# FNet mixer on one core: the reads of the third and seventh block products stand in a row on VectorE, and the work for the other token half moves behind the second group's weight sums

## The chip, the cores and the metric

The kernel runs on one core of a Trainium2 chip. The metric is the device time of one execution in microseconds (us). The time before is the median of three runs, 673.58 us (673.05 to 673.78). The profile is of one further execution, which took 673.93 us from start to end; the span from its first to its last instruction is 672.2 us, so 1.73 us lie around the span.

## The reference, cut to what matters

```python
xn = _layernorm(x)                        # x: 2048 tokens x 512
a = einsum("bsd,ed->bse", xn, hid_re)     # DFT along the hidden axis
b = einsum("bsd,ed->bse", xn, hid_im)
s = einsum("ts,bse->bte", seq_re, a) - einsum("ts,bse->bte", seq_im, b)
y = _layernorm(xn)
h = gelu(einsum("bsd,df->bsf", y, w1) + b1)     # 512 -> 1792
g = silu(einsum("bsf,fd->bsd", h, w2) + b2)     # 1792 -> 512
return x + s * g
```

All inputs are fp32. The kernel writes an fp32 factor as a rounded high part and a rest (`hi`, `lo`) and forms each product as three matmuls: high by high, high by rest, rest by high.

## The kernel before, in words

The program is one stream of calls in a fixed order. Each engine (TensorE, VectorE, ScalarE, GpSimd and the DMA queue of SyncE) takes its own instructions in the order in which the calls were written, and waits on semaphores where an operand is missing or a buffer is still being read. So where a call stands in the code sets what stands ahead of it on its engine.

It has four stages, one behind the other on TensorE: the DFT along the hidden axis (to some 95 us of the span), the first MLP layer (`h_product`, line 646), the second MLP layer (`m_product`), and the DFT along the sequence (`multiply_by`). The change lies in the last part of the first stage and at the start of the second.

**The block products of the first stage.** The 2048 tokens are four blocks of 512. For blocks 2 and 3 the hidden DFT is done in the manner of Strassen and Winograd: seven block products p in the order 1, 2, 5, 6, 3, 7, 4, written by `q_product` (line 540). Each has four chunks c of 128 tokens, and a chunk is six matmuls into one PSUM accumulator: `qy`, `qx` or `qz`, by p. Products 1, 6, 7 and 4 of one chunk share the accumulator `qy`. Behind products 1, 5, 6 and 4 ScalarE copies the accumulator out (line 520); behind 2, 3 and 7 VectorE adds it to what was copied before (line 525, called by `post`). These reads must be over before the next product adds to the same accumulator: chunk c of product 4 waits for VectorE's read of chunk c of product 7.

`q_product` takes one list of steps for each chunk. They are calls for what later work needs, and are written behind the chunk: the next group's weights and the token operands of the first MLP layer.

**The weights.** The first MLP layer also uses seven products, for each of seven weight groups j. `w1_load` brings a group by DMA into `w1r`, `w1_sums` (lines 437 to 440) makes four sums in place on VectorE, `w1_round` (444) makes the high parts on ScalarE and `w1_rest` (83) the rests on VectorE. There is one buffer for `w1r`, so the load of group j+1 waits for the rests of group j. Loads 1 and 2 are issued by GpSimd.

**The token operands.** They are seven per token half tau: "11", "12", "21", "22" and the sums t1 to t4, for tau 1 (blocks 2 and 3, used in the block products too) and tau 0 (blocks 0 and 1). `y_scale` (461) scales one on VectorE, `y_sum` (475) makes a sum in place on VectorE, `y_round` (79) rounds on ScalarE and `y_rest` (83) makes the rest on VectorE.

**The start of the first MLP layer.** `h_seq` sets the order: groups 0 and 1 with tau 1 alone, then both with tau 0, then the other groups with both halves. With (j, p) for group and product, the first thirteen are (0,1), (0,5), (0,6), (0,2), (0,3), (0,7), (1,1), (1,5), (0,4), (1,6), (1,2), (1,3), (1,7), each six matmuls; the next, (0,1) with tau 0, is the first that reads a token operand of tau 0. Products 1, 6, 7 and 4 of a group share the accumulator `hy`, and 5 and 3 share `hz`. Behind 1, 5 and 6 ScalarE copies the accumulator out (`hc`, `hu`, line 671); behind 2, 3 and 7 VectorE adds it (lines 700, 706, 710) and ScalarE applies the GELU (660). `y_late` lists the calls that are written ahead of a given product of this order; the key's last number is tau.

## Time and profile before

| | |
|---|---|
| median of three runs | 673.58 us (673.05 to 673.78) |
| the profiled execution | 673.93 us |
| its span | 672.2 us |
| mean granted TensorE clock | 0.995 |
| bytes moved by DMA | 172.28 MB |
| sequence-DFT loads `c<-ct` by SyncE | 68 of 512 KB, 5.8 us each |

The rows of TensorE are modelled: a matmul's row is 0.39 us long, while the next starts 0.23 us behind it, so the distance from start to start is what counts. A row of the timeline holds its start and its length in us, the engine, the source line, the operation, out<-in, and in brackets the idle time ahead of it and what ended it.

### The profile page before, as it was taken

The page shows a single profiled execution, that of the slowest core. Times are in us where ns is not written, and L with a number is a line of the kernel's source. Part 1 is how long each engine was busy: PE and PEld are TensorE (multiplying, and loading weights), DVE is VectorE, ACT ScalarE, POOL GpSimd, SP SyncE. Part 2 cuts the span into 40 slices and gives each one's busy share as a digit, 9 for nine tenths or more (in the row PEclk, how much of TensorE's full clock was granted, in tenths as well). Part 3 has the DMA queues.
Part 4 walks back from the last instruction along what each step waited for, and adds up shares of the span by engine and source line. Part 5 has one row for each costly group of instructions (what it writes and reads, how often), then busy time and mean ns, then how long its engine had stood idle before and what let it go on. Part 6 is the DMA issues. An engine that isn't in the chain of part 4 may idle for free.

```text
span 672.2 us, 8165 instructions
## 1 busy us (share of the span) xinstructions
PE 663.4 (99%) x2908; PEld 544.5 (81%) x2908; DVE 544.0 (81%) x592; ACT 355.1 (53%) x395; POOL 50.7 (8%) x84
## 2 busy tenths in 40 slices
PE   9999989999999999999999999999999999999996
PEld 5888877888888888888888888888888888888885
DVE  7999886667778856987888999729978299998985
ACT  4745656544555665555456455446445455646540
POOL 1001000222112100000000100000000001210100
PEclk9999989999999999999999999999999999999999
DMA  8879260597998999798799997416555558996873
GB/s 319 268 250 231 94 233 1 221 332 273 331 341 302 417 417 362 261 394 292 276 376 409 390 324 255 157 34 206 182 155 142 128 126 264 302 258 255 294 253 126
DMA packets 70329, 172.28 MB, mean 256 GB/s; under 512 B 6640, under 2 KB 21008, under 8 KB 70288
## 3 DMA queue, kind: packets, MB, share of 16 engines
q1 hardware_dynamic: 57904, 131.36, 55.4%
q0 software_dynamic: 12032, 39.86, 18.9%
q10 hardware_dynamic: 352, 0.54, 0.3%
q8 instruction: 23, 0.38, 0.2%
q14 instruction: 18, 0.15, 0.1%
HBM read 121.38 MB, written 50.35 MB: 255 GB/s over the span
## 4 chain that ended last, share of the span: by engine, by line
PE 93%; DVE 4%; ACT 1%; issue 1%; DMA 0%; DVEq 0%; ACTq 0%
PE pz L841 19%; PE px L841 18%; PE ma L841 11%; PE hy L655 11%; PE mb L841 8%; PE pd L338 6%; PE hz L655 5%; PE pw L841 5%; PE hx L655 3%; PE px L1160 2%; PE pw L1160 2%; PE qy L537 1%; PE pd L353 1%; DVE q L525 1%; DVE xT L475 1%
## 5 line engine op out<-in xcount | busy, mean ns | idle before, releaser
L947 DVE TENSOR_TENSOR c<-c,c 128x1024 f32<-128x1024 f32 x32 | 39.0, 1219 | 4.4 <-DMA c<-ct 4.4
L65 DVE TENSOR_TENSOR R_b1l<-c,R_b1h 128x1024 fp32r<-128x1024 f32 x16 | 19.5, 1222 | 13.7 <-ACT R_b1h L64 10.4
L660 ACT ACTIVATE hc<-hc,b_t 128x1024 f32<-128x1024 f32 (+1 forms) x18 | 17.3, 962 | 24.7 <-DVE hc L700 19.7
L64 ACT ACTIVATE R_s3h<-c 128x1024 fp32r<-128x1024 f32 x16 | 17.0, 1061 | 24.2 <-DVE c L947 15.9
L841 PE MATMUL pw<-R_s1h,L 128*128 128x512 f32 x96 | 29.7, 389 | 0.0
L83 DVE TENSOR_TENSOR w1l<-w1r,w1h 128x1792 fp32r<-128x1792 f32 x7 | 14.2, 2024 | 18.3 <-ACT w1h L444 18.3
L64 ACT ACTIVATE R_b2h<-c 128x1024 fp32r<-128x1024 f32 x16 | 16.9, 1057 | 22.0 <-DVE c L952 17.5
L65 DVE TENSOR_TENSOR R_s2l<-c,R_s2h 128x1024 fp32r<-128x1024 f32 x16 | 19.6, 1223 | 8.6 <-PE pz L841 8.6
L64 ACT ACTIVATE R_s2h<-c 128x1024 fp32r<-128x1024 f32 x16 | 17.0, 1060 | 16.7 <-PE px L841 9.3
L65 DVE TENSOR_TENSOR R_s3l<-c,R_s3h 128x1024 fp32r<-128x1024 f32 x16 | 19.5, 1219 | 3.8 <-PE pz L841 3.8
L64 ACT ACTIVATE R_s1h<-c 128x1024 fp32r<-128x1024 f32 x16 | 16.4, 1051 | 11.3 <-DVE c L958 11.3
L955 POOL DMA_DIRECT2D c<-ct x8 | 7.0, 875 | 200.7 <-DVE c L952 162.5
L64 ACT ACTIVATE R_b1h<-c 128x1024 fp32r<-128x1024 f32 x16 | 16.6, 1052 | 10.1 <-PE px L841 4.4
L64 ACT ACTIVATE R_a1h<-c 128x1024 fp32r<-128x1024 f32 x16 | 16.9, 1054 | 8.9 <-PE pz L841 7.2
L841 PEld LDWEIGHTS pw<-R_s1h,L 128*128 128x128 f32 x96 | 18.0, 188 | 3.8
L65 DVE TENSOR_TENSOR R_b2l<-c,R_b2h 128x1024 fp32r<-128x1024 f32 x16 | 19.4, 1218 | 1.5 <-PE px L841 1.5
L65 DVE TENSOR_TENSOR R_a1l<-c,R_a1h 128x1024 fp32r<-128x1024 f32 x16 | 19.5, 1221 | 1.3 <-PE px L841 1.1
L952 DVE TENSOR_TENSOR c<-c,c 128x1024 f32<-128x1024 f32 x16 | 19.6, 1222 | 0.4
L65 DVE TENSOR_TENSOR R_s4l<-c,R_s4h 128x1024 fp32r<-128x1024 f32 x16 | 19.5, 1219 | 0.5 <-PE px L841 0.4
L64 ACT ACTIVATE R_s4h<-c 128x1024 fp32r<-128x1024 f32 x16 | 16.8, 1050 | 4.8 <-PE pz L841 2.9
L65 DVE TENSOR_TENSOR R_s1l<-c,R_s1h 128x1024 fp32r<-128x1024 f32 x16 | 18.8, 1219 | 0.1
L64 ACT ACTIVATE w2h<-w 128x1024 fp32r<-128x1024 f32 (+1 forms) x14 | 13.2, 943 | 10.8 <-DVE w L768 3.9
(950 smaller groups left out, 2221.3 us busy)
## 6 DMA issues: line engine op xcount, KB each, us to landing
c<-ct SPq DMA_DIRECT2D x68, 512.0 KB, 5.8
m<-h_d SPq DMA_DIRECT2D x48, 512.0 KB, 6.8
h_d<-ht POOLq DMA_DIRECT2D x21, 512.0 KB, 6.1
s_d<-sa SPq DMA_DIRECT2D x32, 256.0 KB, 3.9
la<-s_d SPq DMA_DIRECT2D x32, 256.0 KB, 6.1
h_d<-hc POOLq DMA_DIRECT2D x13, 512.0 KB, 3.6
x<-x SPq DMA_DIRECT2D x16, 256.0 KB, 4.7
sa<-a_d SPq DMA_DIRECT2D x8, 512.0 KB, 5.8
```

The costliest lines, as they stand in the source:

```text
L64: nc.scalar.activation(hi, src, AF.Copy)
L65: nc.vector.tensor_sub(lo, src, hi.bitcast(F32))
L83: nc.vector.tensor_sub(hi_lo[1], src, hi_lo[0].bitcast(F32))
L338: nc.tensor.matmul(acc, xt[i, k][px], weights[m * NK + k][pw], start=n == 0, stop=n == len(terms) - 1)
L353: nc.tensor.matmul(dacc[0, m], xt[0, k][px], weights[m * NK + k][pw], start=seen[m] == 0, stop=seen[m] == 3 * NK - 1)
L655: nc.tensor.matmul(acc[:, tau, :], w[:, W1_AT[p], k * P:(k + 1) * P], r[:, k, :], start=p in (1, 5, 2) and i == 0, stop=p in (2, 3, 4) and ...
L660: nc.scalar.activation(dst, src, AF.Gelu_apprx_tanh, bias=b1_t[:, row:row + 1])
L841: nc.tensor.matmul(acc[k][:, tau, :], a, c[:, tau, :], start=first and i == 0, stop=last and i == len(terms) - 1, skip_group_check=True)
L947: nc.vector.tensor_sub(t, t, raw)
L952: nc.vector.tensor_add(raw, raw, t)
L955: nc.gpsimd.dma_start(out=t, in_=ct[1, 1, n], accum_op=ALU.add)
L1160: nc.tensor.matmul(acc[KEY[name]][k][:, tau, :], a[k], c[:, tau, :], start=False, stop=u == us[-1] and i == 2, skip_group_check=True)
```

## The change

Four calls are edited, all of them lists of steps; no operation is added or taken away.

- In products 3 and 7 the steps between the reads are gone: VectorE reads product 3's four accumulators and product 7's four one behind the other. Only `w1_sums(1)` is left, behind the last.
- What stood between is queued later: `y_scale(1, 1)`, `y_rest("11", 0)` and `y_sum("t1", 0)` behind those sums, in product 4; `w1_round(1)` behind product 4's last chunk.
- In `y_late` the rounding of t1, `w1_rest(1)` and `w1_load(2)` are written ahead of (0,5), and the chain of tau 0's operands follows in a new distribution; `w1_sums(2)` and t4's sum, rounding and rest move into the products of tau 0.

```diff
-    q_product(3, [post(3, 0), then(y_round, "11", 0)], [post(3, 1), then(y_scale, 1, 1)], [post(3, 2), then(y_rest, "11", 0)],
-              [post(3, 3), then(y_sum, "t1", 0)])
-    q_product(7, [post(7, 0), then(y_round, "t1", 0)], [post(7, 1), then(w1_sums, 1)], [post(7, 2), then(y_rest, "t1", 0)],
-              [post(7, 3), then(w1_round, 1)])
-    q_product(4, [then(w1_rest, 1), then(w1_load, 2)], [then(y_sum, "t2", 0)], [], [then(y_scale, 1, 0)])
+    q_product(3, [post(3, 0), then(y_round, "11", 0)], [post(3, 1)], [post(3, 2)], [post(3, 3)])
+    q_product(7, [post(7, 0)], [post(7, 1)], [post(7, 2)], [post(7, 3), then(w1_sums, 1)])
+    q_product(4, [then(y_scale, 1, 1), then(y_rest, "11", 0)], [then(y_sum, "t1", 0)], [], [then(w1_round, 1)])
...
-    y_late = {(0, 5, 1): [then(y_round, "t2", 0)],
-              (0, 6, 1): [then(y_rest, "t2", 0)],
-              (0, 3, 1): [then(y_round, "21", 0)],
-              (0, 7, 1): [then(y_rest, "21", 0)],
-              (1, 5, 1): [then(y_round, "22", 0)],
+    y_late = {(0, 5, 1): [then(y_round, "t1", 0), then(w1_rest, 1), then(w1_load, 2)],
+              (0, 6, 1): [then(y_rest, "t1", 0), then(y_sum, "t2", 0)],
+              (0, 2, 1): [then(y_round, "t2", 0), then(y_scale, 1, 0)],
+              (0, 3, 1): [then(y_rest, "t2", 0), then(y_round, "21", 0)],
+              (1, 5, 1): [then(y_rest, "21", 0), then(y_round, "22", 0)],
               (1, 6, 1): [then(y_rest, "22", 0), then(y_sum, "t3", 0)],
               (1, 2, 1): [then(y_round, "t3", 0)],
-              (1, 3, 1): [then(y_rest, "t3", 0), then(w1_sums, 2)],
-              (1, 7, 1): [then(y_sum, "t4", 0)],
-              (0, 5, 0): [then(y_round, "t4", 0)],
-              (0, 6, 0): [then(y_rest, "t4", 0)]}
+              (1, 3, 1): [then(y_rest, "t3", 0)],
+              (0, 1, 0): [then(w1_sums, 2)],
+              (0, 5, 0): [then(y_sum, "t4", 0)],
+              (0, 6, 0): [then(y_round, "t4", 0)],
+              (0, 2, 0): [then(y_rest, "t4", 0)]}
```

Three places show how this moves the instructions. A row holds the source line, the operation, out<-in and the size; + is a row of the changed kernel, - one of the kernel before. The first is VectorE while TensorE works on products 3 and 7; `qz` rows read product 3, `qy` rows product 7.

```order
 L525 SCALAR_TENSOR_TENSOR q_0_849<-qz_795,qq,q_0_849 128x512
-L461 TENSOR_TENSOR xT_1_237<-xT_1_237,rowR_674 128x1024
 L525 SCALAR_TENSOR_TENSOR q_2_869<-qz_808,qq,q_2_869 128x512
-L83 TENSOR_TENSOR y_0l<-xT_0_676,y_0h 128x1024
 L525 SCALAR_TENSOR_TENSOR q_2_869<-qz_821,qq,q_2_869 128x512
-L475 TENSOR_TENSOR xT_0_676<-xT_0_235,xT_0_676 128x1024
 L525 SCALAR_TENSOR_TENSOR q_0_792<-qy_694,nq,q_0_792 128x512
 L525 SCALAR_TENSOR_TENSOR q_0_792<-qy_707,nq,q_0_792 128x512
+L525 SCALAR_TENSOR_TENSOR q_2_815<-qy_716,nq,q_2_815 128x512
+L525 SCALAR_TENSOR_TENSOR q_2_815<-qy_729,nq,q_2_815 128x512
```

A scaling, a rest and a sum of 128x1024 no longer stand ahead of the first read of product 7 (`qy_694`), and the last two reads of it stand ahead of the weight sums.

The second is VectorE behind those sums, to the first products of the first MLP layer; `w1l` are the rests of weight group 1, `yt_0l` those of t1 and t2, and `hc` the first VectorE addition of the MLP layer.

```order
+L461 TENSOR_TENSOR xT_1_237<-xT_1_237,rowR_674 128x1024
+L83 TENSOR_TENSOR y_0l<-xT_0_676,y_0h 128x1024
+L475 TENSOR_TENSOR xT_0_676<-xT_0_235,xT_0_676 128x1024
+L83 TENSOR_TENSOR w1l_994<-w1r_883,w1h_993 128x1792
 L83 TENSOR_TENSOR yt_0l<-xT_0_676,yt_0h 128x1024
-L525 SCALAR_TENSOR_TENSOR q_2_815<-qy_729,nq,q_2_815 128x512
-L83 TENSOR_TENSOR w1l_964<-w1r_883,w1h_963 128x1792
 L475 TENSOR_TENSOR xT_0_676<-xT_1_237,xT_0_676 128x1024
 L461 TENSOR_TENSOR xT_1_680<-xT_1_680,rowR_674 128x1024
+L698 TENSOR_TENSOR hc_1056<-hc_1056,hx_1090 128x512
 L83 TENSOR_TENSOR yt_0l<-xT_0_676,yt_0h 128x1024
```

The weight rests now stand ahead of t1's rests, and the addition of product (0,2) ahead of t2's rests.

The third is ScalarE from the end of product 6's copies to the second copy of the MLP layer; `q` rows copy product 4 out, `w1h` is the rounding of weight group 1, and `hc` the copy of product (0,1).

```order
+L520 ACTIVATE q_0_962<-qy_694,nq 128x512
+L520 ACTIVATE q_0_962<-qy_707,nq 128x512
+L520 ACTIVATE q_2_982<-qy_716,nq 128x512
+L520 ACTIVATE q_2_982<-qy_729,nq 128x512
+L444 ACTIVATE w1h_993<-w1r_883 128x1792
+L669 ACTIVATE hc_1056<-hy_1049 128x512
 L79 ACTIVATE yt_0h<-xT_0_676 128x1024
-L444 ACTIVATE w1h_963<-w1r_883 128x1792
-L520 ACTIVATE q_0_972<-qy_694,nq 128x512
-L520 ACTIVATE q_0_972<-qy_707,nq 128x512
-L520 ACTIVATE q_2_993<-qy_716,nq 128x512
-L520 ACTIVATE q_2_993<-qy_729,nq 128x512
```

The rounding of weight group 1 moved from ahead of product 4's four copies to behind them, directly ahead of the copy of product (0,1); t1's rounding moved behind that copy.

## The prediction

> **What bounds the kernel.** First the page: how busy each engine is, and who makes up the chain that ended last.

> ```profile
> PE 663.4 (99%) x2908; PEld 544.5 (81%) x2908; DVE 544.0 (81%) x592; ACT 355.1 (53%) x395; POOL 50.7 (8%) x84
> ...
> PE 93%; DVE 4%; ACT 1%; issue 1%; DMA 0%; DVEq 0%; ACTq 0%
> ```

> TensorE has no rest, and DMA is nowhere on the chain. Only time in which TensorE stands, or runs slowly, can be won. So next the waits of TensorE; a row gives the waiting line, whom it waited for, the total, the number and the longest.

> ```profile
> PE qy L537 <- DVE q L525: 1.8, 1, 1.8
> PE idle_ps L194 <- DVE warm L229: 1.2, 1, 1.2
> PE hy L655 <- DVE hc L710: 0.3, 1, 0.3
> PE pt L262 <- DVE xc L252: 0.2, 1, 0.2
> ```

> That is the whole list. The first and the third lie where the code is edited. The timeline of TensorE around both, from the last matmul of product 7:

> ```profile
> 85.54 0.39 PE L537 MATMUL qy<-A7h,yt_1l 128*128 128x512 f32 x1
> 87.71 0.73 PE L537 MATMUL qy<-W,yt_1h 128*128 128x512 f32 x2 [1.78 <-DVE q L525]
> ...
> 94.70 0.39 PE L537 MATMUL qy<-W,yt_1l 128*128 128x512 f32 x1
> 94.93 0.39 PE L655 MATMUL hy<-y_1h,w1h 128*128 128x512 f32 x1
> ...
> 112.61 0.39 PE L655 MATMUL hy<-y_0h,w1h 128*128 128x512 f32 x1
> ...
> 115.10 0.39 PE L655 MATMUL hz<-yt_0h,w1l 128*128 128x512 f32 x1
> 115.77 0.50 PE L655 MATMUL hy<-yt_1h,w1h 128*128 128x512 f32 x1 [0.28 <-DVE hc L710]
> ...
> 118.64 0.39 PE L655 MATMUL hx<-y_0h,w1h 128*128 128x512 f32 x1
> ```

> The pace: from 94.93 to 112.61 stand 13 products of six matmuls, so 17.68 / 78 = 0.227 us from start to start. Product 4 should have begun at 85.54 + 0.23 = 85.77 and began at 87.71: 1.94 us lost. Its 24 matmuls should take 5.44 us, and the next product begins 7.22 us later: 1.78 us more. The windows tell why (the row's end holds the granted clock, the DMA share and GB/s):

> ```profile
> 85.50:87.70 2.20, 0.43 (x2) 0.01 (x1) 2.20 (x4) 0.67 (x1) 0.00 (x0) 1.00 0.89 339
> 87.70:89.20 1.50, 1.49 (x6) 1.27 (x7) 1.50 (x4) 0.39 (x1) 0.00 (x0) 0.94 0.46 173
> 89.20:92.40 3.20, 3.20 (x9) 2.42 (x9) 3.17 (x6) 2.51 (x3) 0.00 (x0) 0.50 0.44 165
> ```

> Some 1.5 us behind the wait the clock is granted at half, for about 3.3 us. The stall therefore costs 1.94 + 1.78 = **3.72 us**. The small one at 115.10 costs 118.64 - 115.10 less 13 x 0.227, **0.59 us**: 0.44 of waiting and 0.15 of slower matmuls behind it.

> [...]

> **Part 1, the reads in a row.** VectorE at that place:

> ```profile
> 80.88 1.41 DVE L525 SCALAR_TENSOR_TENSOR q<-qz,qq,q 128x512 f32<-128x512 f32 x2
> 82.20 1.21 DVE L461 TENSOR_TENSOR xT<-xT,rowR 128x1024 f32<-128x1024 f32 x1
> ...
> 83.99 1.21 DVE L83 TENSOR_TENSOR y_0l<-xT,y_0h 128x1024 fp32r<-128x1024 f32 x1
> ...
> 85.78 1.21 DVE L475 TENSOR_TENSOR xT<-xT,xT 128x1024 f32<-128x1024 f32 x1
> 86.92 1.40 DVE L525 SCALAR_TENSOR_TENSOR q<-qy,nq,q 128x512 f32<-128x512 f32 x2
> 88.24 0.41 DVE L437 TENSOR_TENSOR w1r<-w1r 128x256 f32<-128x256 f32 x1
> ...
> 89.70 0.74 DVE L525 SCALAR_TENSOR_TENSOR q<-qy,nq,q 128x512 f32<-128x512 f32 x1
> 90.36 1.22 DVE L83 TENSOR_TENSOR yt_0l<-xT,yt_0h 128x1024 fp32r<-128x1024 f32 x1
> 91.49 0.74 DVE L525 SCALAR_TENSOR_TENSOR q<-qy,nq,q 128x512 f32<-128x512 f32 x1
> 92.15 2.01 DVE L83 TENSOR_TENSOR w1l<-w1r,w1h 128x1792 fp32r<-128x1792 f32 x1
> 94.09 1.22 DVE L475 TENSOR_TENSOR xT<-xT,xT 128x1024 f32<-128x1024 f32 x1
> ```

> VectorE waits for nothing here: it is behind because three operations of 128x1024 stand ahead of the first read of product 7 (86.92). From start to start a read takes 0.66 (91.49 to 92.15), such an operation 1.13 (90.36 to 91.49), the weight rests 1.94, the four sums 1.46 (88.24 to 89.70).

> Without the three, product 3's reads run from 80.88 to 83.52. Product 7's chunk 0, whose last matmul starts 18 paces ahead of 85.54 (81.46), is read until 84.26, 1.5 us before product 4 can begin; chunk 3's read starts when its sum is in, 0.43 us after the last matmul started (94.70 in the timeline, 95.13 in ScalarE's rows below), at 85.97. It is needed at 85.77 + 18 x 0.227 = 89.85. So TensorE goes from product 7 into product 4 without a pause, and the clock has no reason to fall: product 4 ends at 91.21 instead of 94.93. **Gain 3.72 us.**

> **Part 2, the weight rounding behind product 4's copies.** ScalarE before:

> ```profile
> 73.73 1.84 ACT L520 ACTIVATE q<-qy,qq 128x512 f32<-128x512 f32 x3
> ...
> 89.81 1.70 ACT L444 ACTIVATE w1h<-w1r 128x1792 fp32r<-128x1792 f32 x1 [1.72 <-DVE w1r L440]
> 91.42 1.44 ACT L520 ACTIVATE q<-qy,nq 128x512 f32<-128x512 f32 x2
> ...
> 95.13 0.69 ACT L520 ACTIVATE q<-qy,nq 128x512 f32<-128x512 f32 x1 [0.69 <-PE qy L537]
> 96.49 0.60 ACT L671 ACTIVATE hc<-hy 128x512 f32<-128x512 f32 x1 [0.67 <-PE hy L655]
> 96.98 1.05 ACT L79 ACTIVATE yt_0h<-xT 128x1024 fp32r<-128x1024 f32 x1
> 97.93 0.59 ACT L671 ACTIVATE hc<-hz 128x512 f32<-128x512 f32 x1
> ...
> 99.83 1.28 ACT L660 ACT_TABLE_LOAD   x1
> 101.29 0.73 ACT L660 ACTIVATE hc<-hc,b_t 128x512 f32<-128x512 f32 x1 [0.18 <-DVE hc L700]
> 101.92 1.05 ACT L79 ACTIVATE y_0h<-xT 128x1024 fp32r<-128x1024 f32 x1
> ```

> Now the last copy of product 4 starts 0.43 behind its last matmul (90.98), at 91.41; the copies in a row stand 0.58 apart (73.73), so the rounding starts at 91.99, the copy of (0,1) 1.61 later at 93.60 (89.81 to 91.42), and that ends at 94.20. Product (0,6) adds to the accumulator that this copy reads and is due two products behind 91.21, at 93.93. It starts at about 94.25: **a new wait of 0.32 us**. With the slow restart of 0.15 seen at 115.77 it costs 0.47. The bounds: nothing, if the rounding starts 0.3 earlier, and 0.8 if each of the handovers is 0.1 longer.

> **Part 3, the tail of the chain.** On VectorE the sums now end at 88.09, the scaling, the rest and t1's sum at 91.5, and `w1l` waits for the rounding until 93.7: 2.1 us of VectorE's time, which nothing needs at once. The rests of group 1 are in at 95.8; (1,1) is due at 91.21 + 6 x 1.36 + 0.47 = 99.84, so that is covered (1.36 is six paces, one product). Behind them come t1's rest, t2's sum and a scaling (3.4 us and 0.1 for operations that use each other's result), (0,2)'s addition, t2's rest, and the additions of (0,3) and (0,7), at a read's 0.66 each, so the last ends near 102.3. Product (0,4) needs that at 91.21 + 8 x 1.36 + 0.47 = 102.56: **a cover of 0.2 us**. ScalarE does t2's rounding from 98.2, the table load (1.28), a GELU (0.63), a rounding (0.95), two GELUs and the copy of (1,1), done at 103.8; (1,6) needs it at 103.92: **a cover of 0.1 us**. I cost both at nothing. Bounds: a gain is excluded, as no wait is left there before; the loss is a microsecond of TensorE for each microsecond that the chain slips beyond its cover.

> **Part 4, the second stall.** At 115.10 TensorE waited for (1,7)'s addition. The weight sums of group 2 and t4's sum now stand behind that addition, not ahead; (1,7)'s last matmul starts near 109.1, and its addition, with t3's rest ahead of it, ends near 110.5; (1,4) is due 15 products behind 91.21, at 112.1. **Gain 0.59 us.**

> **Part 5, DMA.** The loads and stores are the same. Load 1 of the weights and the window behind:

> ```profile
> w1r<-w POOLq DMA_DIRECT2D x1, 512.0 KB, 4.6
> ...
> 100.00:125.00 25.00, 24.72 (x110) 20.12 (x109) 15.73 (x21) 16.13 (x23) 0.87 (x2) 1.00 0.06 22
> ```

> Its issue at 81.3 and 4.6 us give a landing near 85.9, and the sums want it at 86.63. The stores of products 3 and 7 now fall nearer to it, so it may land later; up to 88.7 the idle time of VectorE in part 3 hides that. Load 2 waits for `w1l`, now at 95.8, and its sums stand behind 110. Between 100 and 125 us the DMA engines are 6% busy, so no backlog crosses, and what follows starts from the same state, only earlier: the gain stays to the end.

> **The sum.** 3.72 + 0.59 - 0.47 = 3.84 us. The profiled execution would go from 673.93 to 670.1; the median shown is 0.35 lower, so 673.58 - 3.84 = **669.7 us**.

> **Rivals.**
> 1. *The thin covers break.* VectorE and ScalarE hand work to each other some ten times between 91 and 104 us; a slip of 0.1 each uses up both covers. For it: 0.1 us is less than I can read off rows. Against: VectorE has idle time as soon as it has caught up. Waits of 0.5 to 1.5 us in (0,4) or (1,6) give 670.2 to 671.2. Were a wait to pass the point between 0.28 and 1.78 us where the clock falls, 1.78 come on top: about 673.
> 2. *The half clock has another cause.* Then 1.94 + 0.59 - 0.47 = 2.06 is won: 671.5. Against it: the fall follows the longest wait of the list, and the window from 100 to 125 us (part 5), with the short wait in it, reads 1.00.
> 3. *Slower: the weight load lands late.* If it lands after about 88.9, the sums, `w1h`, `w1l` and all behind them slip one for one into (0,4) and (1,6). A wait of 2.5 us, with the fall of the clock, eats the whole 4.3 us: that is a landing at 91.4, 10.1 us after its issue. At 13 us the wait is 5.4, and the time 673.58 - 4.31 + 5.4 + 1.78 = 676.5. Against it: 4.6 us before.
> 4. *The change doesn't do what it says*: a read of product 7 still stands behind a rest or a DMA, and the time stays at 673.6. The order on VectorE speaks against it.

> **How the numbers follow.** Forecast 62% (its own range 669.2, with no new wait, to 670.2), rival 1 in its mild form 20%, in its hard form 4%, rival 2 5%, rival 3 5%, rival 4 4%. The range 669.0 to 671.6 takes in the forecast, the mild form and rival 2. A measurement of this kernel can tell about 0.2%, 1.3 us, from no change. Faster by more: 62 + 20 + 5 = 87%; within: the hard form and rival 4, 8%; slower: rival 3, 5%.

> **What would show it.** Right: no wait of `qy` L537 for `q` L525 and a clock of 1.00 through product 4; the first matmul of line 655's successor near 91.2; a wait of some 0.3 us for ScalarE's `hc` two products later; none at (1,4). Wrong: a wait of `hy` for `hc` of a microsecond or more in 100 to 105 us (rival 1), half a clock without a wait (rival 2), VectorE's sums late on a DMA (rival 3).

## The result, and the profile after

| | before | after |
|---|---|---|
| median of six runs | 673.36 us (673.05 to 674.34) | 670.74 us (670.33 to 671.17) |
| profiled execution, its span | 673.93 us, 672.2 us | 670.9 us, 669.1 us |
| mean granted TensorE clock in it | 0.995 | 0.998 |

The ratio is 0.9959, with a 95% interval of 0.9946 to 0.9972: faster by 0.4%, 2.6 us between the medians. The forecast was 3.84 us; the time lies in the stated range of 669.0 to 671.6 us, but above the forecast's own band of 669.2 to 670.2.

First the page of the changed kernel, its busy line and its chain, and then the waits of TensorE:

```profile
PE 661.0 (99%) x2908; PEld 543.0 (81%) x2908; DVE 544.1 (81%) x592; ACT 354.7 (53%) x395; POOL 50.7 (8%) x84
...
PE 97%; DMA 1%; DVE 1%; ACT 0%; issue 0%; SPq 0%; DVEq 0%
```

```profile
PE idle_ps L194 <- DVE warm L229: 1.2, 1, 1.2
PE pd L353 <- ACT W L290: 1.2, 1, 1.2
PE pt L262 <- DVE xc L252: 0.2, 1, 0.2
PE pd L353 <- ACT xt L64: 0.2, 1, 0.2
```

VectorE's share of the chain went from 4% to 1%, and both waits that the change aimed at are gone from the list. What is left lies in the first 10 us. The waits of 0.3 us that had been forecast are too short for this list, since a row of TensorE is modelled 0.39 us long; they show in the timeline of TensorE, and in the list for its weight loads, where two waits for ScalarE's `hc` stand:

```profile
86.19 0.39 PE L537 MATMUL qy<-A7h,yt_1l 128*128 128x512 f32 x1
86.41 0.62 PE L537 MATMUL qy<-W,yt_1h 128*128 128x512 f32 x2
...
91.85 0.39 PE L653 MATMUL hy<-y_1h,w1h 128*128 128x512 f32 x1
...
94.35 0.39 PE L653 MATMUL hz<-yt_1h,w1l 128*128 128x512 f32 x1
94.87 0.50 PE L653 MATMUL hy<-yt_1h,w1h 128*128 128x512 f32 x1
...
96.36 0.39 PE L653 MATMUL hx<-y_1h,w1h 128*128 128x512 f32 x1
...
104.29 0.39 PE L653 MATMUL hy<-yt_1h,w1l 128*128 128x512 f32 x1
104.63 0.50 PE L653 MATMUL hy<-yt_1h,w1h 128*128 128x512 f32 x1
...
115.64 0.39 PE L653 MATMUL hx<-y_0h,w1h 128*128 128x512 f32 x1
```

```profile
PEld hy L653 <- ACT hc L669: 0.9, 2, 0.6
```

Product 4 begins one pace behind product 7 (86.19 to 86.41) and its 24 matmuls take 5.44 us. Then (0,6) begins 0.52 us behind the matmul ahead of it instead of 0.23, and (1,6) 0.34 us.

**A measure that leaves the start of the kernel out.** Call *the stretch* the time from the last matmul of product 7 to the first of (0,2) with tau 0. At full pace it is 127 x 0.2267 = 28.8 us. It was 118.64 - 85.54 = 33.10 us in the profile before, and is 115.64 - 86.19 = **29.45** after: 3.65 us less. From the stretch's end to the end of the span it is 553.56 before (672.2 - 118.64) and 553.46 after, so the gain stays, as forecast. But the stretch began 0.65 us later in the profile after, at 86.19 against 85.54, in code that is the same (0.64 us of it are there at the first matmul of product 2 already, at 58.57 and 59.21, ahead of the first edited call), and the medians differ by 2.6 us, not by 3.65. The experiments ask where that microsecond is.

### The profile page after: what moved, and what is told of

It reads as the page before. It is cut to its first block, busy times and chain, and to the rows that moved or that the text cites. A ratio compares the mean times of both kernels' runs of the same rounds, so it can differ in the third digit from the quotient of the medians.

```text
span 669.1 us, 8164 instructions
## 1 busy us (share of the span) xinstructions
PE 661.0 (99%) x2908; PEld 543.0 (81%) x2908; DVE 544.1 (81%) x592; ACT 354.7 (53%) x395; POOL 50.7 (8%) x84
## 4 chain that ended last, share of the span: by engine, by line
PE 97%; DMA 1%; DVE 1%; ACT 0%; issue 0%; SPq 0%; DVEq 0%
PE pz L840 20%; PE px L840 18%; PE ma L840 11%; PE hy L653 11%; PE mb L840 9%; PE pd L338 6%; PE hz L653 5%; PE pw L840 5%; PE qy L537 3%; PE hx L653 3%; PE px L1159 2%; PE qz L537 2%; PE pw L1159 2%; DMA rw<-wt 1%; PE qx L537 1%; DVE W L291 0%
## 5 line engine op out<-in xcount | busy, mean ns | idle before, releaser
L83 DVE TENSOR_TENSOR w1l<-w1r,w1h 128x1792 fp32r<-128x1792 f32 x7 | 14.2, 2026 | 20.3 <-ACT w1h L444 20.3
## 6 DMA issues: line engine op xcount, KB each, us to landing
c<-ct SPq DMA_DIRECT2D x68, 512.0 KB, 5.5
m<-h_d SPq DMA_DIRECT2D x48, 512.0 KB, 7.0
h_d<-ht POOLq DMA_DIRECT2D x21, 512.0 KB, 6.9
h_d<-hc POOLq DMA_DIRECT2D x13, 512.0 KB, 3.9
sa<-a_d SPq DMA_DIRECT2D x8, 512.0 KB, 5.8
```

The lines of the kernel that those rows point to most:

```text
L83: nc.vector.tensor_sub(hi_lo[1], src, hi_lo[0].bitcast(F32))
```

## The experiments

**Where is the missing microsecond?** The first two are the two kernels themselves.

> The kernel before, unchanged, to see how one execution differs from the next. In the two profiles the stretch from the last matmul of product 7 to product (0,2) of the other token half is 3.65 us shorter after the change (33.10 against 29.45), but the medians differ by 2.6 us only, and the profiled execution of the changed kernel came 0.65 us later to product 7. Theory A (the start varies): this profile shows the stall of 1.8 us and 3.3 us of half clock again, the stretch at 33.1 +- 0.1, and the last matmul of product 7 somewhere from 85.4 to 86.4. Theory B (the length of the half clock varies): the last matmul of product 7 stays at 85.5, and the stretch differs from 33.1 by more than 0.3. The ratio to itself is 1.000 within 0.0015.

> The changed kernel, unchanged. Theory A: the stretch is 29.45 +- 0.1 again, the start moves by up to 1 us from one profile to the next, and the ratio comes near 0.995 to 0.996. Theory B: the same stretch, since there is no half clock here; the spread of its times is smaller than that of the kernel before.

The kernel before took 673.99 us (11 runs, ratio to itself 0.9996, 0.9987 to 1.0006); the changed kernel 670.73 (5 runs, ratio 0.9951, 0.9937 to 0.9965). Both stretches came out as in the first profiles: 118.87 - 85.73 = 33.14, and 115.62 - 86.17 = 29.45. The start does move, so A held for these two profiles. But the list of all executions showed what neither profile could: the kernel before has two groups. In its first 41 listed executions the mean granted clock was 0.995 to 0.997 in 16, with spans near 672.5 us, and 0.998 or more in 25, with spans near 671.4. The changed kernel's eleven all had 0.998 or more. (A fall to a half for 3.4 us takes 0.0025 off the mean. In the changed kernel's profile, which has no half clock ahead of it, what is missing from 1.000 lies behind the last matmul, which starts at 663.49: the clock falls at 666.6 us of the 669.1.) So theory B, of which neither profile showed a sign, had to be asked again, with the kernel before profiled in an execution of the second group:

> The kernel before, unchanged, for one more profile. In the timed executions of the kernel before so far the mean granted clock is 0.995 to 0.997 in 16 of 41 (spans near 672.5) and 0.998 to 1.000 in the others (spans near 671.4). Theory (the wait of 1.8 us makes the clock fall in some executions only; in the others TensorE, at full speed, waits a second time, for the read of product 7's last chunk, as the kernel with added matmuls does): a profile with a clock of 0.998 or more has the wait of 1.8 us, no half clock, a wait of 0.3 to 0.4 us at product 4's last chunk, and a stretch of 31.9; one of 0.995 to 0.997 has 33.1 as before. Rival (the half clock is there in every execution, and spans differ by their start alone): 33.1 whatever the mean clock.

> The same again, as some six in ten executions show no fall of the clock: a stretch of 31.9 with a mean clock of 0.998 or more, or 33.1 with 0.995 to 0.997.

Both profiles fell into that group (mean clock 1.000). TensorE's timeline of the first:

```profile
85.81 0.39 PE L537 MATMUL qy<-A7h,yt_1l 128*128 128x512 f32 x1
87.97 0.73 PE L537 MATMUL qy<-W,yt_1h 128*128 128x512 f32 x2 [1.77 <-DVE q L525]
...
92.01 0.40 PE L537 MATMUL qy<-W,yt_1l 128*128 128x512 f32 x1
92.54 0.74 PE L537 MATMUL qy<-W,yt_1h 128*128 128x512 f32 x2
...
94.05 0.39 PE L655 MATMUL hy<-y_1h,w1h 128*128 128x512 f32 x1
...
117.76 0.39 PE L655 MATMUL hx<-y_0h,w1h 128*128 128x512 f32 x1
```

And its windows behind the wait (granted clock third from the right), ahead of the same windows of the first repeated profile of the kernel before:

```profile
88.00:89.50 1.50, 1.50 (x7) 1.24 (x8) 1.50 (x4) 0.34 (x1) 0.00 (x0) 1.00 0.49 183
89.50:92.70 3.20, 3.06 (x14) 2.11 (x13) 3.17 (x6) 2.63 (x3) 0.00 (x0) 1.00 0.42 160
```

```profile
87.90:89.40 1.50, 1.50 (x6) 1.24 (x7) 1.50 (x4) 0.38 (x1) 0.00 (x0) 0.98 0.49 183
89.40:92.60 3.20, 3.20 (x9) 2.48 (x8) 3.17 (x6) 2.60 (x3) 0.00 (x0) 0.50 0.43 162
```

The wait is the same, 1.77 us, but no half clock follows. TensorE then runs ahead into a second wait, for VectorE's read of product 7's last chunk (92.01 to 92.54):

```profile
91.74 0.74 DVE L525 SCALAR_TENSOR_TENSOR q<-qy,nq,q 128x512 f32<-128x512 f32 x1
```

That read ends at 92.48. Product 4 takes 94.05 - 87.97 = 6.08 us: neither 5.44 nor the 7.22 of the half clock. The stretch is 117.76 - 85.81 = **31.95**; in the second profile it is 117.90 - 85.97 = 31.93. So the half clock followed this wait in two of four profiles, and it costs 33.1 - 31.9 = 1.2 us net, since without it 0.6 us is lost at the later read. Of the 58 executions of the kernel before that have a listed clock, 23 are at 0.997 or below (median span 672.6 us) and 35 above (671.4): the same 1.2 us. The gain of the change is therefore 31.94 - 29.45 = 2.5 us in the larger group and 3.65 in the smaller, 3.0 in the mean. The mean spans of these 58 executions and of the changed kernel's eleven, 671.97 and 668.88 us, differ by 3.1, so over many executions the changed kernel's stretch does not start later, and the 0.65 us were chance as far as these show. The medians of the runs differ by 2.6 to 2.8, as the median before lies in or near the larger group.

**Is it the idle time that makes the clock fall?** The kernel before with harmless matmuls in the wait:

```diff
+    def fill():
+        t = bank("fill")
+        for q in range(8):
+            nc.tensor.matmul(t, idle[:, :P], idle, start=True, stop=True)
...
-              [post(7, 3), then(w1_round, 1)])
+              [post(7, 3), then(w1_round, 1), fill])
```

> The kernel before with eight more matmuls of a zero bf16 tile into a free accumulator between products 7 and 4 (they compute nothing that is used). TensorE then has work while it waits for the read of product 7. Theory (the 3.3 us of half clock come from the idle time): product 4 starts as late as before or up to 0.3 us later, the clock stays at 1.00, the stretch is 31.3 to 31.6 in place of 33.1, and the time 1.5 to 1.8 us under that of the kernel before. Rival (the half clock has another cause, or comes from the lateness of the read): the clock falls to a half as before, the stretch is 33.1 to 33.4.

```profile
86.72 1.90 PE L619 MATMUL fill<-idle 128*128 128x512 bf16 x8
88.67 0.73 PE L537 MATMUL qy<-W,yt_1h 128*128 128x512 f32 x2
...
92.70 0.40 PE L537 MATMUL qy<-W,yt_1l 128*128 128x512 f32 x1
93.25 0.73 PE L537 MATMUL qy<-W,yt_1h 128*128 128x512 f32 x2
```

Product 4 starts as late as before, yet the mean clock is 0.998 or more in all ten executions; with four in ten as the share of falls, ten without one have a chance of 0.6%. The second wait is there (92.70 to 93.25), which the expectation had missed: the stretch is 118.44 - 86.50 = 31.94, as in the kernel before without the fall, not 31.3 to 31.6. The median time, 673.33 us, is only 0.15 under the kernel before, 673.48 in the runs beside it (ratio 0.9993, 0.9984 to 1.0002): the time saved of 1.5 to 1.8 us was a miss, as it was reckoned against executions with the fall, and even against those the stretch is only 1.2 us shorter, as the second wait gives part of it back.

**How long must the wait be?** The changed kernel with additions on an unused tile ahead of product 7's first read, five of them and seven:

```diff
+    delay = consts.tile([P, W // 2], F32, name="delay")
+    nc.gpsimd.memset(delay, 0.0)
...
-    q_product(3, [post(3, 0), then(y_round, "11", 0)], [post(3, 1)], [post(3, 2)], [post(3, 3)])
+    q_product(3, [post(3, 0), then(y_round, "11", 0)], [post(3, 1)], [post(3, 2)],
+              [post(3, 3)] + [then(nc.vector.tensor_add, delay, delay, delay)] * 5)
```

> The changed kernel with five additions of 128x256 on an otherwise unused tile ahead of the first read of product 7 on VectorE (about 0.45 us each, 2.25 us in all, of which the 1.5 us of slack hide the first part). Theory (the half clock comes from the wait, and needs one longer than a point between 0.28 and 1.78 us): TensorE loses 0.8 us at product 4; whether the clock falls tells on which side of 0.6 us of idle time the point lies. Rival (the half clock has nothing to do with the wait): the clock stays at 1.00 here, as it does in the changed kernel, or falls in both.

> As the kernel with five additions ahead of the first read of product 7, with seven. With five the wait was 0.55 us of idle time and the clock stayed at 1.00. With seven the wait is 1.3 to 1.5 us. Theory (a wait makes the clock fall when it is long enough; the point lies between 0.55 and 1.78 us): product 4 loses 1.5 to 1.7 us at its start, and either the clock reads 1.00 behind it (the point lies above 1.4) or a half for some 3.3 us, 1.7 us more (it lies below). Rival (the half clock has another cause): 1.00.

> The changed kernel with seven additions ahead of the first read of product 7, timed: a wait of 1.47 us, which left the clock alone in its one profile. Theory (the fall depends on how the wait lies to a window that runs by itself, so a wait of 1.5 us makes it fall in a smaller share of executions than one of 1.8): mean clocks of 0.995 to 0.997 in none or few of the executions, against four in ten for the kernel before. Rival (a wait of this length is as bad as one of 1.8 us): four in ten again, and times that differ by 1.7 us between the two groups.

The first row is that of five additions, the second of seven:

```profile
86.88 0.73 PE L537 MATMUL qy<-W,yt_1h 128*128 128x512 f32 x2 [0.55 <-DVE q L525]
```

```profile
87.80 0.74 PE L537 MATMUL qy<-W,yt_1h 128*128 128x512 f32 x2 [1.47 <-DVE q L525]
```

Neither profile shows a half clock. The stretches are 116.26 - 85.94 = 30.32 and 117.20 - 85.94 = 31.26, so the waits cost 0.87 and 1.81 us over the changed kernel's 29.45: product 4 starts 0.71 and 1.63 us late, and the matmuls behind lose another 0.16 and 0.18. In the third run, the kernel with seven additions took 672.59 us (11 runs) with a clock of 0.998 or more in each. With the 23 in 58 of a wait of 1.78 us, eleven in eleven would have a chance of 0.4%. So with the wait of 1.47 us no fall was seen in twelve executions, and with one of 1.78 in 23 of 58.

**In which executions does it fall?** The traces that were kept answer this. Rows of 0.1 us give the edges of the half clock to some 0.01 us; the first three are of the first profile of the kernel before, the fourth of the one whose timeline stands above.

```profile
89.00:89.10 0.10, 0.10 (x2) 0.10 (x1) 0.10 (x1) 0.00 (x0) 0.00 (x0) 0.56 0.96 348
92.40:92.50 0.10, 0.10 (x2) 0.10 (x1) 0.10 (x1) 0.10 (x1) 0.00 (x0) 0.87 0.00 0
669.20:669.30 0.10, 0.00 (x0) 0.00 (x0) 0.00 (x0) 0.00 (x0) 0.00 (x0) 0.89 0.91 348
```

```profile
670.90:671.00 0.10, 0.00 (x0) 0.00 (x0) 0.00 (x0) 0.00 (x0) 0.00 (x0) 0.69 0.33 82
```

The half clock lasts from 89.01 to 92.43, 3.413 us in the trace's own record, and the full clock behind it 576.852 us, 169 times as long, until it falls again behind the last matmul. The other profile with a half clock has the same two figures. In the eleven profiles without one the full clock lasts 662.186 or 665.599 us from its first record up to that last fall, 194 or 195 times 3.4133. So in these profiles the changes of the clock lie whole numbers of 3.413 us apart, and steps of that length can be counted back to the wait from the last fall (669.28 and 670.94 in the rows above).

Counted back so, the steps sort the profiles. In the two with the half clock the whole wait of 1.78 us lies in one step (85.60 to 89.01, and 85.92 to 89.33), and the clock falls at that step's end. In the two without it an end of a step, at 87.26 and 87.25, cuts the wait into 1.06 and 0.71 us, and into twice 0.89. With seven additions the wait of 1.47 us lies whole in one step in both profiles, and the clock does not fall. That fits the theory of the last expectation as far as these six profiles go; it was read from them afterwards, and no run tests it by itself. If a wait of 1.78 us could lie anywhere in the steps, it would be uncut with a chance of (3.41 - 1.78) / 3.41, some 48%, an estimate from these two lengths alone, to be set against the 23 of 58, 40%.

**Do the new waits come from the weight rounding?** The changed kernel with the rounding of weight group 1 two copies earlier:

```diff
-    q_product(4, [then(y_scale, 1, 1), then(y_rest, "11", 0)], [then(y_sum, "t1", 0)], [], [then(w1_round, 1)])
+    q_product(4, [then(y_scale, 1, 1), then(y_rest, "11", 0)], [then(w1_round, 1), then(y_sum, "t1", 0)], [], [])
```

> The changed kernel with the rounding of weight group 1 between the second and the third copy of product 4 on ScalarE, where its sums have just come in. Theory (the two new waits, of 0.29 and 0.11 us and their slow restarts, 0.66 us in all, both come from this rounding standing directly ahead of the copy of (0,1)): both waits are gone, VectorE has no 2 us of idle time ahead of the weight rests, the stretch is 28.8 us, and the time is 0.6 to 0.7 us under that of the changed kernel (ratio to it 0.999). Rival (the second wait comes from the hand-overs between VectorE and ScalarE alone): only the wait at (0,6) goes, 0.43 us, and (1,6) still waits for its copy. Rival (the copies of product 4's last two chunks, now 1.6 us later, hold up (0,5)): a new wait of up to 0.5 us for a copy at (0,5).

> The kernel with the rounding of weight group 1 ahead of product 4's last two copies, again. The stretch is 28.8 us as in its first profile, the span the start plus 28.8 plus 553.5, and the time 0.3 to 0.7 us under the changed kernel's 670.73. If the later start of the changed kernels (85.94 to 86.19 against 85.54 and 85.73 for the last matmul of product 7) is chance, this profile may show 85.5; if it belongs to them, 85.9 to 86.2 again, and the profile of the kernel before with added matmuls 85.5 to 85.8.

ScalarE around the rounding, in the first of the two profiles; the changed kernel's rows of the same place stand in the next section.

```profile
89.13 0.69 ACT L520 ACTIVATE q<-qy,nq 128x512 f32<-128x512 f32 x1 [0.67 <-PE qy L537]
89.72 1.70 ACT L444 ACTIVATE w1h<-w1r 128x1792 fp32r<-128x1792 f32 x1
91.31 1.25 ACT L520 ACTIVATE q<-qy,nq 128x512 f32<-128x512 f32 x2
93.21 0.60 ACT L669 ACTIVATE hc<-hy 128x512 f32<-128x512 f32 x1 [0.65 <-PE hy L653]
```

The copy `hc` now waits for TensorE (0.65 us), not TensorE for it. The stretches are 114.77 - 85.98 = 28.79 and 114.69 - 85.91 = 28.78: TensorE at full pace throughout, so both waits had come from that rounding, and neither rival holds. The times are 670.24 us (ratio to the kernel before 0.9946, 0.9933 to 0.9959) and 670.11 (0.9943, 0.9930 to 0.9957). That is 0.5 to 0.6 us under the changed kernel's 670.73; the two intervals overlap, and it is the stretch, 0.66 us shorter in each of two profiles, that shows the gain. It is the best version found. The starts, 85.98 and 85.91, tell nothing new: over all profiles that were taken the last matmul of product 7 lies anywhere from 85.54 to 86.50, the latest in a kernel made from the one before.

**What removed the second stall?** The changed kernel with the later weight sums back:

```diff
-              (1, 3, 1): [then(y_rest, "t3", 0)],
-              (0, 1, 0): [then(w1_sums, 2)],
-              (0, 5, 0): [then(y_sum, "t4", 0)],
-              (0, 6, 0): [then(y_round, "t4", 0)],
-              (0, 2, 0): [then(y_rest, "t4", 0)]}
+              (1, 3, 1): [then(y_rest, "t3", 0), then(w1_sums, 2)],
+              (1, 7, 1): [then(y_sum, "t4", 0)],
+              (0, 5, 0): [then(y_round, "t4", 0)],
+              (0, 6, 0): [then(y_rest, "t4", 0)]}
```

> The changed kernel with the weight sums of group 2, and t4's sum, rounding and rest, back at the places that they had before. Theory (the second stall of the kernel before went because these no longer stand ahead of (1,7)'s addition): a wait for that addition at (1,4) is back, and longer than the 0.44 us of the kernel before, as VectorE is later here: the addition would end 2.6 us later than now, near 114.0, with product (1,4) due at 112.9, so 1.1 us of waiting and 0.15 of slow restart; the stretch is 30.7. Rival (the earlier start of the MLP layer alone undid it): no wait there, 29.45.

```profile
114.30 0.50 PE L653 MATMUL hy<-yt_1h,w1h 128*128 128x512 f32 x1 [1.04 <-DVE hc L708]
```

The wait is back, 1.04 us of idle time, and the stretch is 117.19 - 86.36 = 30.83 (30.7 expected). Without that edit the change would have given back 1.4 of its 3.65 us.

## Why the prediction was right, and what it mis-sized

**What bounds, and part 4: right.** TensorE waits nowhere behind the start but for the two short waits; the second stall is gone, and putting the sums back brings it back.

**Part 1, the reads in a row: the mechanism right, the size not that of a usual execution.** VectorE's rows after the change:

```profile
81.52 2.72 DVE L525 SCALAR_TENSOR_TENSOR q<-qz,qq,q 128x512 f32<-128x512 f32 x4
84.16 2.06 DVE L525 SCALAR_TENSOR_TENSOR q<-qy,nq,q 128x512 f32<-128x512 f32 x3
86.61 0.75 DVE L525 SCALAR_TENSOR_TENSOR q<-qy,nq,q 128x512 f32<-128x512 f32 x1 [0.40 <-PE qy L537]
...
94.37 2.03 DVE L83 TENSOR_TENSOR w1l<-w1r,w1h 128x1792 fp32r<-128x1792 f32 x1 [2.01 <-ACT w1h L444]
```

With the 0.65 us of the later start, these are the forecast's 80.88, 83.52 and 85.97, and VectorE waits 2.0 us for the rounding, against 2.1 forecast. The term of 3.72 us holds against the profiled execution, which has the half clock. But its part of 1.78 us is absent in 35 of 58 executions, and where it is absent TensorE loses 0.6 us to the read of the last chunk: against most executions the term is 1.93 + 0.64 = 2.57 (87.97 against 85.81, and 6.08 against 5.44). This is the step that missed: a cost seen in one profile was carried over to the median. The profile gave a hint, its execution being 0.35 us above the median of those shown; the prediction only subtracted it. Of the 1.2 us between forecast and measured gain this is nearly all. That the time still fell into the range was in part luck: 670.74 us stands among the times of rival 1's mild form, 670.2 to 671.2, but that form wanted a wait of 0.5 to 1.5 us, and the one that came cost 0.24 (part 3).

**Rival 2** (the half clock has another cause) is refuted by the kernel with added matmuls: with the wait filled, the clock fell in none of ten executions. In the kernel before, with the wait of 1.78 us, it fell in 23 of 58.

**Part 2, the copy behind the rounding: right.** ScalarE:

```profile
92.05 0.69 ACT L520 ACTIVATE q<-qy,nq 128x512 f32<-128x512 f32 x1 [0.67 <-PE qy L537]
92.64 1.70 ACT L444 ACTIVATE w1h<-w1r 128x1792 fp32r<-128x1792 f32 x1
94.23 0.59 ACT L669 ACTIVATE hc<-hy 128x512 f32<-128x512 f32 x1
...
98.82 1.06 ACT L79 ACTIVATE yt_0h<-xT 128x1024 fp32r<-128x1024 f32 x1 [1.66 <-DVE xT L475]
99.90 1.28 ACT L658 ACT_TABLE_LOAD   x1
101.20 0.73 ACT L658 ACTIVATE hc<-hc,b_t 128x512 f32<-128x512 f32 x1
...
104.00 0.58 ACT L669 ACTIVATE hc<-hy 128x512 f32<-128x512 f32 x1
```

The copy of (0,1) ends at 94.82 and (0,6) starts at 94.87: 0.29 us of waiting (0.52 less one pace) against 0.32 forecast. By the start of (0,2) it costs 0.43 us with the slow restart, 96.36 against 91.85 + 18 x 0.2267 = 95.93; the forecast was 0.47.

**Part 3, the thin covers: one of them did not hold, rival 1 in small.** (1,6) waited 0.11 us and restarted 0.13 slower, 0.24 where nothing had been costed. The copy ends at 104.58, or 103.93 without the later start, 0.13 us behind the forecast's 103.8: the table load starts 1.08 us behind the rounding ahead of it (98.82 to 99.90), where the forecast had 0.95, the distance of two instructions that overlap (96.98 to 97.93 in the profile before). The rest is a hand-over of 0.05 us behind the copy (104.58 to 104.63), which the forecast had at nothing, and a product that is due 0.05 earlier, as (0,6) lost less. The other cover, at (0,4), held. With the rounding two copies earlier this wait is gone as well, so it hung on the same late rounding.

**Part 5, DMA: right.** The load of group 1, in the changed kernel's profile:

```profile
w1r<-w POOLq DMA_DIRECT2D x1, 512.0 KB, 4.6
```

It landed 4.6 us behind its issue, as before, so rival 3 had no ground. Rival 4 is excluded by the order and by the result.

The sum, then: against the profile with the half clock 3.72 + 0.59 - 0.43 - 0.24 = 3.64 us, and 3.65 measured in the stretch; against one without it, 2.57 + 0.59 - 0.43 - 0.24 = 2.49, and 2.5 measured.

## What to carry to other kernels

Ahead of a chain of waits, look at what stands in the queue of the engine that must release the next step: here three operations that nobody needed yet held up TensorE for 1.9 us. When they are moved, everything that the waiting engine will ask for next moves closer, so the next thin cover has to be found too: the rounding that went to the end of the copies made two new waits, and two places earlier it made none. And where the list of executions shows a mean clock or a span in two groups, price a stall from both, since one profile shows one of them.
